# Polysketch attention and multiplicative FFN: the written order of all engines carried on to the third group's x

## The chip, the cores and the metric

One core of a Trainium2 chip runs the kernel. Its engines are TensorE (PE, matmuls and transposes), VectorE (DVE), ScalarE (ACT), GpSimd (POOL) and SyncE (SP), which here issues the DMAs. Each engine works through its own queue in order; an instruction waits in its queue until the tiles it reads are written and the buffers it writes are free. The metric is the device time of one execution in microseconds (us).

## The reference

For 4 batches, 4 heads, 1088 positions and head dimension 32, with two sketch matrices S1 and S2 of 8 x 32:

```
phi(x)[.., i*8+j] = (S1 x)[i] * (S2 x)[j]            # 64 features
kv  = sum over s of phi(k)[s] v[s];  z = sum over s of phi(k)[s]
att = (phi(q) kv) / (phi(q) z + 1e-6)
x   = att as (4*1088, 128)                            # heads side by side
out = ((x @ w1) * (x @ w2)) @ w3 @ w_out              # d_ff = 1024
```

w1, w2, w3 and w_out arrive as float64 and are read as 64-bit words; the kernel turns them into float32 itself.

## The kernel before

**Fold.** Nothing non-linear stands between w3 and w_out, so the kernel computes w3o = w3 @ w_out once and then needs only ((x @ w1) * (x @ w2)) @ w3o. w3 is 1024 x 1024 and comes in 16 chunks of 128 x 512 (two to each block of 128 rows), behind w1 and w2 (two chunks each) and w_out (two chunks). A chunk in its raw form is 512 KB; there are six buffers for raw chunks, and the step that reads chunk n issues the load of chunk n+6 on SP.

**Converting one chunk** (`convert`, L256): `words` are two ACT instructions (L269 writes cv_c, L270 writes cv_m; two buffers each), `join` two DVE instructions (L281, L282), `add` one (L285). For w3 the result is a tile w3c (three buffers). `w3_t` (L415) turns it with four PE transposes (L421) and copies them to w3T with ACT (L423). When both halves of a row block are there, `w3_mm` (L425) makes one block of w3o with eight PE matmuls (L428) and an ACT copy (L429).

**Attention side.** `k_steps(b)` makes, for batch b, the small matrices that the q side needs: a maximum and two-part split of k (`lead`: peak, first, second on DVE), two transposes and a feature product (`k_feat_by_head`: tr on DVE, ab on PE and DVE, feat on DVE), sums over positions on PE (`g_sum`, `kv_sum`, and the rest rows), then a chain of small steps in which DVE and PE alternate: fin1 (DVE), T on PE, a pair split on DVE, N on PE, a pair split on DVE, and the transposed kv block kz. `next_in` issues the loads of later batches. `q_main(b, half)` makes x for one group of 512 positions: transpose and grid on DVE, lead on ACT, rest, ay1 and ay2 on PE, then split, dens, dens2 and phi on DVE, phT (eight PE transposes L807, two ACT copies L809) and nd (PE L818, ACT copy L822 to xT).

**FFN side.** There are nine groups (eight of 512 positions, one of 256). For each of 8 chunks of 128 columns, `ffn_ab` (L858) does a = w1 x on PE (L862), its copy on ACT (L864), b = w2 x on PE (L866) and the product ab on DVE (L868). `ffn_o` (L871) adds w3o[c] ab to the group's output on PE (L875); behind the eighth, DVE transposes the result to oT (L879) and SP stores it. a, b, the w3 transposes and the w3o product share three PSUM banks (tag "h"); the output has one bank ("out"), and so have the T, N, kz, k_ab and x products ("t").

**Order.** Up to the eighth chunk of group 0 all instructions have an order written out in a list (`run_all`, L945); ordering edges on each engine make the queues follow it. Everything behind it is traced from `merge`, which mixes lists of steps by the costs written beside them, and the framework's planner then arranges each engine's instructions by its own cost estimates and by when buffers come free; all of it is behind the written part on its engine. The first such mix is group 1's FFN chunks, the K steps of batch 1 and the rest of the w3 conversion and fold; the second is the pending output products, down to four, and x of group 2 (`q_main(1, 0)`).

Of the kernel before, what the change touches and what calls it, by code (L numbers as in the profile page):

```python
# [33 lines left out]
def kernel(  # L34
# [26 lines left out]
    NC = DF // 128  # L61
# [98 lines left out]
    def load_raw(n):  # L160
        while n_raw[0] < min(n, len(chunks)):
            i = n_raw[0]
            n_raw[0] += 1
            raw[i] = io.tile([128, CW], I64, tag="raw", bufs=NRAW, name="raw")
            if i == 2:

                nc.vector.memset(raw[i].bitcast(I32)[:1, :1], 0)
            src = chunk_src(*chunks[i])
            dst = raw[i]
            if len(src.shape) == 3:  # L170
                dst = dst.rearrange("p (c d) -> p c d", d=DM)
            nc.sync.dma_start(dst, src)
# [50 lines left out]
    def halves(words, n):  # L223

        w = words.bitcast(I32)
        return bview(w, [[2, n]]), bview(w[:, 1:], [[2, n]])
# [29 lines left out]
    def convert(n, dst, signs=True):  # L256

        x = {}

        def words():
            for name in "cm":
                x[name] = work.tile([128, CW], F32, tag="cv_" + name, name="cv_" + name)
            lo, hi = halves(raw.pop(n), CW)
            nc.scalar.mul(x["c"], hi.bitcast(F32), 2.0 ** -112)  # L269
            nc.scalar.mul(x["m"].bitcast(I32), lo.bitcast(U32), 2.0 ** -29)  # L270
            load_raw(n + 1 + NRAW)
            if signs:
                x["s"] = zeros_with_signs(x["c"], 128, CW)

        def join():
            x["t"] = t = dst().bitcast(I32)
            c = x["c"].bitcast(I32)
            if signs:
                nc.vector.scalar_tensor_tensor(t, c, 3, x["s"], ALU.logical_shift_left, ALU.bitwise_or)
            else:  # L280
                nc.vector.tensor_scalar(t, c, 3, 0x7FFFFFF8, ALU.logical_shift_left, ALU.bitwise_and)  # L281
                nc.vector.scalar_tensor_tensor(t, c, -(1 << 31), t, ALU.bitwise_and, ALU.bitwise_or)  # L282

        def add():
            nc.vector.tensor_tensor(x["t"], x["t"], x["m"].bitcast(I32), ALU.add)  # L285
        return [words, join, add]

    def run_all(steps):
        for f in steps:
            f()  # L290
# [115 lines left out]
    def w_in_steps():  # L406
        return [convert(n, lambda name=name, i=i: {"w1": w1, "w2": w2}[name][:, i * CW:(i + 1) * CW])
                for n, (name, i) in enumerate(chunks) if name in ("w1", "w2")]

    def w_out_steps():  # L410

        tiles = []
        w3T, w3c = {}, {}

        def w3_t(i):  # L415
            ko, half = divmod(i, NH)
            if half == 0:
                w3T[ko] = work.tile([128, NC, 128], F32, tag="w3T", name="w3T")
            ps = psum.tile([128, CW // 128, 128], F32, tag="h", bufs=3, name="ps_wt")
            for c in range(CW // 128):  # L420
                nc.tensor.transpose(ps[:, c], w3c[i][:, c * 128:(c + 1) * 128], ident)  # L421
            c0 = half * (CW // 128)
            nc.scalar.copy(w3T[ko][:, c0:c0 + CW // 128], ps)  # L423

        def w3_mm(ko):  # L425
            ps = psum.tile([128, DM], F32, tag="h", bufs=3, name="ps_w3o")
            for c in range(NC):
                nc.tensor.matmul(ps, w3T[ko][:, c], wo[:, c], start=(c == 0), stop=(c == NC - 1))  # L428
            nc.scalar.copy(w3o[:, ko], ps)  # L429

        for n, (name, i) in enumerate(chunks):
            after = []
            if name == "wo":
                c = CW // DM
                dst = lambda i=i, c=c: wo[:, i * c:(i + 1) * c].rearrange("p c d -> p (c d)")
            elif name == "w3":
                dst = lambda i=i: w3c.setdefault(i, work.tile([128, CW], F32, tag="w3c", bufs=3, name="w3c"))
                after.append((0.5, lambda i=i: w3_t(i)))
                if i % NH == NH - 1:
                    after.append((0.9, lambda ko=i // NH: w3_mm(ko)))  # L440
            else:
                continue
            words, join, add = convert(n, dst, signs=False)
            tiles.append(([(0.6, words)], [(0.4, join), (0.3, add)], after))
        st = []
        for k in range(len(tiles) + 2):
            for part, lag in ((0, 0), (1, 1), (2, 2)):
                if 0 <= k - lag < len(tiles):
                    st += tiles[k - lag][part]
        return st  # L450

# [92 lines left out]
    def rest_steps(m):  # L546
        kf = k_rs[m]
        return k_feat(lambda: [kf.rearrange("p h d -> p (h d)")], 1, k_rest[m], "t" if m else "wb")[0]
# [277 lines left out]
    def q_main(b, half):  # L826
        def transpose(qT):
            t = by_head["q", b]
            nc.vector.transpose(qT, t[:, half * 512:(half + 1) * 512])
            if half == 1:  # L830
                nc.vector.transpose(qT_rest[:, b * SR:(b + 1) * SR], t[:, SM:])
                if b + 2 < B:
                    load_by_head("q", b + 2)
        return q_steps((b, half), transpose, lean=2 * b + half < 3)

    def q_rest():
        return q_steps("rest")
# [33 lines left out]
    def ffn_o(g, c):  # L871
        _, n, dst = groups[g]
        if c == 0:
            o_ps[g] = psum.tile([DM, 512], F32, tag="out", name="ps_o")
        nc.tensor.matmul(o_ps[g][:, :n], w3o[:, c], ab_sb.pop((g, c))[:, :n], start=c == 0, stop=c == NC - 1)  # L875
        if c == NC - 1 and g < NG - 1:

            oT = work.tile([128, 512], F32, tag="oT", name="oT")
            nc.vector.transpose(oT, o_ps[g])  # L879
            dst(oT)  # L880
# [15 lines left out]
    pend = []  # L896

    def ffn_steps(g, left):

        st = []  # L900
        if g is not None:
            for c in range(NC):
                st.append((1.7 * groups[g][1] / 512, lambda c=c: ffn_ab(g, c)))
                pend.append((g, c))
                while len(pend) > left:
                    st += o_step(*pend.pop(0))
        while len(pend) > left:
            st += o_step(*pend.pop(0))
        return st
# [6 lines left out]
    def merge(*streams):  # L916
        streams = [x for x in streams if x]
        tot = [sum(c for c, _ in x) for x in streams]
        done = [0.0] * len(streams)
        pos = [0] * len(streams)  # L920
        res = []
        while any(pos[i] < len(x) for i, x in enumerate(streams)):
            i = min((i for i, x in enumerate(streams) if pos[i] < len(x)),
                    key=lambda i: (done[i] + streams[i][pos[i]][0] / 2) / max(tot[i], 1e-9))
            res.append(streams[i][pos[i]])
            done[i] += res[-1][0]
            pos[i] += 1
        return res

    def run(steps):  # L930
        for _, f in steps:
            f()

    w_in, w_out = w_in_steps(), w_out_steps()
    fs = lambda steps: [f for _, f in steps]
    (peak, first, second, nat0, tr0, ab0, kp0, gs0, kv0, nat1, tr1, ab1, kp1, gs1, kv1, gr, kvr,
     fin1, next_in, T_mm, T_pair, N_mm, N_pair, kz) = fs(k_steps(0))
# [1 line left out]
    q_tr, q_grid, q_lead, q_rem, ay1, ay2, split, dens, dens2, phi, phT, nd = fs(q_main(0, 0))  # L939
    n_tr, n_grid, n_lead, n_rem, n_ay1, n_ay2, n_split, n_dens, n_dens2, n_phi, n_phT, n_nd = fs(q_main(0, 1))  # L940
    f = fs(ffn_steps(0, 16))
    (v0, j0, a0), (v1, j1, a1), (v2, j2, a2), (v3, j3, a3) = w_in
    pause = lambda n: lambda: idle(n)
    out_st, w_out = fs(w_out[:7]), w_out[7:]
    run_all([sk_words, sketch_pairs, nat0, nat1, peak, sketch_T, tr0, tr1, ab0, ab1, r_nat, r_tr, first, second,  # L945
             gs0, r_ab, kp0, gs1, kp1, gr, r_kp, sketch_P_mm, kv0, kv1, kvr, q_tr, pause(5),
             sketch_R, sketch_Pa, fin1, load_more, next_in, T_mm, sketch_Pb, kz, pause(13), T_pair, N_mm, q_grid, q_lead,
             pause(16), N_pair, ay1, q_rem, v0, v1, ay2, n_tr, pause(30), split, dens, dens2, phi, j0, a0, j1, a1,
             phT, nd, n_grid, n_lead, n_rem, f[0], n_ay1, n_ay2, v2, n_split, j2, a2, f[1], v3, f[2], j3, a3, n_dens, f[3],
             out_st[0], n_dens2, f[4], out_st[1], n_phi, f[5], *out_st[2:4], f[6], n_phT, n_nd, *out_st[4:7], f[7]])  # L950
    traced = nc.cur_bb.bb.instructions
    first_part = len(traced)
    run(merge(ffn_steps(1, 16), k_steps(1), w_out))
    run(merge(ffn_steps(None, 4), q_main(1, 0)))
    run(merge(ffn_steps(2, 6), q_main(1, 1), rest_steps(1) + k_steps(2)))
    run(merge(ffn_steps(3, 6), q_main(2, 0)))
    run(merge(ffn_steps(4, 6), q_main(2, 1), k_steps(3)))
    run(merge(ffn_steps(5, 6), q_main(3, 0)))
    run(merge(ffn_steps(6, 6), q_main(3, 1)))
    run(merge(ffn_steps(7, 6), q_rest()))  # L960
    run(ffn_steps(8, 2))
    run(ffn_steps(None, 0))
    last_out()
# [41 lines left out]
```

## Time and profile before

| | |
|---|---|
| three runs | 302.32, 303.18, 300.95 us; median 302.32 |
| the profiled execution | 300.8 us; span in the profile 299.0 us; mean granted clock 0.994 |
| PE | 282.7 us busy (95%), 2214 matmul instructions |
| DVE | 207.6 us (69%), 523 instructions |
| ACT | 117.1 us (39%), 226 |
| POOL | 7.5 us (3%), 12 |
| DMA | 22.37 MB |

The page's second part cuts the span into 40 slices of 7.5 us; a digit is the busy share of an engine in tenths, 9 being 90% or more. PEclk is the clock granted to PE in tenths of full speed. A line of the fifth part gives source line, engine, operation, written and read tiles with their shapes and the number of instructions, then busy time in us, mean ns of one, and the engine's idle time ahead of them with what ended most of it. A timeline line gives start and length in us, engine, source line, operation and tiles, and in brackets the idle time ahead of it and its releaser. The rows of PEld are PE's weight loads. Ends of matmuls are modelled: a pair that forms one 512-column product has 1.02 us in the timeline, while the chain of waits, which follows one start to the next, has 0.86 us for it.

### The profile page before, as it was taken

How to read it: one execution, taken by the hardware profiler on the slowest of the kernel's cores; microseconds unless marked ns; L12 is line 12 of the kernel's file. 1: busy time of each engine (PE TensorE's matmuls, PEld its weight loads, DVE VectorE, ACT ScalarE, POOL GpSimd, SP SyncE). 2: the span in 40 equal slices, each digit the busy share in tenths (PEclk: the TensorE clock that was granted, in tenths of full speed). 3: DMA queues.
4: the chain of work that ended last, by engine and by line, in shares of the span. 5: the costliest groups of instructions: out<-in, count | busy, mean ns of one | idle time of the engine just before them, and what ended most of it. 6: DMA issues, size and time to landing. Idle time of an engine off the chain costs nothing.

```text
span 299.0 us, 5582 instructions
## 1 busy us (share of the span) xinstructions
PE 282.7 (95%) x2214; PEld 159.8 (53%) x2214; DVE 207.6 (69%) x523; ACT 117.1 (39%) x226; POOL 7.5 (3%) x12
## 2 busy tenths in 40 slices
PE   7987799589999999999999999999999999999994
PEld 5876343267767774545644435464444444444572
DVE  6989779999998985699579329864862583453131
ACT  4634665667886322320242322122423323223122
POOL 0000000000000010010010001000100000000000
PEclk9999999979999999999999999999999999999999
DMA  5649996456744002200100200020002002002020
GB/s 164 211 99 311 254 309 252 134 160 201 246 123 134 0 2 35 71 2 10 30 0 0 35 2 1 2 37 0 2 0 35 2 0 35 1 2 35 0 35 18
DMA packets 28729, 22.37 MB, mean 75 GB/s; under 512 B 20000, under 2 KB 25248, under 8 KB 28704
## 3 DMA queue, kind: packets, MB, share of 16 engines
q1 hardware_dynamic: 28704, 22.03, 26.8%
q8 instruction: 17, 0.28, 0.4%
q14 instruction: 8, 0.07, 0.1%
HBM read 19.80 MB, written 2.23 MB: 74 GB/s over the span
## 4 chain that ended last, share of the span: by engine, by line
PE 80%; DVE 11%; ACT 3%; DMA 2%; issue 1%; SPq 1%; DVEq 0%
PE ps_o L875 19%; PE a_ps L862 19%; PE b_ps L866 18%; PE ps_kvz L557 5%; PE ps_w3o L428 5%; PE ps_x L818 3%; PE ps_wt L421 2%; PE ps_c L725 2%; PE ps_ph L807 2%; DMA k_sb<-in_k_dram 1%; DMA raw<-in_moe_w_dram 1%; PE ps_ab L504 1%; DVE g_k L301 1%; DVE w3c L285 1%; PE ps_c L738 1%
## 5 line engine op out<-in xcount | busy, mean ns | idle before, releaser
L868 DVE TENSOR_TENSOR ab<-ffa,b_ps 128x512 f32<-128x512 f32 (+1 forms) x72 | 47.1, 655 | 64.7 <-PE b_ps L866 62.9
L864 ACT COPY ffa<-a_ps 128x512 f32<-128x512 f32 (+1 forms) x72 | 40.4, 562 | 98.1 <-PE a_ps L862 98.0
L862 PE MATMUL a_ps<-xT,w 128*128 128x512 f32 (+1 forms) x144 | 71.9, 581 | 1.0 <-ACT xT L822 0.7
L866 PE MATMUL b_ps<-xT,w 128*128 128x512 f32 (+1 forms) x144 | 70.3, 570 | 0.0
L875 PE MATMUL ps_o<-ab,w3o 128*128 128x512 f32 (+1 forms) x144 | 70.0, 582 | 0.1
L866 PEld LDWEIGHTS b_ps<-xT,w 128*128 128x128 f32 x144 | 27.2, 190 | 30.1 <-issue 24.9
L875 PEld LDWEIGHTS ps_o<-ab,w3o 128*128 128x128 f32 x144 | 25.3, 189 | 23.9 <-issue 21.6
L862 PEld LDWEIGHTS a_ps<-xT,w 128*128 128x128 f32 x144 | 24.9, 190 | 23.5 <-issue 14.3
L809 ACT COPY pT<-ps_ph 128x512 f32<-128x512 f32 (+1 forms) x18 | 9.2, 565 | 21.0 <-PE ps_ph L807 21.0
L428 PEld LDWEIGHTS ps_w3o<-wo,w3T 128*128 128x128 f32 x128 | 16.5, 205 | 1.5 <-issue 1.2
L428 PE MATMUL ps_w3o<-wo,w3T 128*128 128x128 f32 x128 | 17.0, 289 | 0.0
L269 ACT ACTIVATE cv_c<-raw 128x512 f32<-128x512 f32 x22 | 14.9, 679 | 2.9 <-DVE w3c L282 1.5
L270 ACT ACTIVATE cv_m<-raw 128x512 int32<-128x512 uint32 x22 | 15.0, 681 | 1.8 <-DVE w3c L285 1.5
L421 PE MATMUL ps_wt<-ident,w3c 128*128 128x128 f32 x64 | 10.2, 288 | 4.7 <-DVE w3c L285 4.7
L215 PE MATMUL idle_ps<-zeros 128*128 128x256 bf16 x88 | 12.7, 309 | 1.7 <-DVE zeros L210 1.7
L822 ACT COPY xT<-ps_x 128x512 f32<-128x512 f32 (+1 forms) x9 | 5.1, 563 | 19.0 <-PE ps_x L818 19.0
L421 PEld LDWEIGHTS ps_wt<-ident,w3c 128*128 128x128 f32 x64 | 7.5, 147 | 8.7 <-ACT cv_c L269 4.2
L215 PEld LDWEIGHTS <-zeros 128*128 128x128 bf16 x88 | 9.6, 112 | 3.8 <-DVE zeros L210 1.7
L701 POOL TENSOR_TENSOR q<-qT,q 128x512 f32<-128x512 f32 x5 | 5.9, 1183 | 208.6 <-ACT q L697 208.6
L423 ACT COPY w3T<-ps_wt 128x512 f32<-128x512 f32 x16 | 9.2, 585 | 4.9 <-PE ps_wt L421 4.6
L807 PEld LDWEIGHTS ps_ph<-ident,ph 128*128 128x128 f32 x68 | 7.9, 142 | 5.8 <-issue 4.0
L285 DVE CUSTOM_DVE_ANT_0 w3c<-w3c,cv_m 128x1024 uint16<-128x1024 uint16 x16 | 10.8, 682 | 0.0
(182 smaller groups left out, 343.9 us busy)
## 6 DMA issues: line engine op xcount, KB each, us to landing
raw<-in_moe_w_dram SPq DMA_DIRECT2D x20, 512.0 KB, 5.0
qh<-in_q_dram SPq DMA_DIRECT2D x4, 544.0 KB, 5.8
k_sb<-in_k_dram SPq DMA_DIRECT2D x4, 512.0 KB, 5.2
out_dram<-oT SPq DMA_DIRECT2D x32, 64.0 KB, 1.9
kh<-in_k_dram SPq DMA_DIRECT2D x12, 128.0 KB, 6.4
v_sb<-in_v_dram SPq DMA_DIRECT2D x12, 128.0 KB, 5.1
raw<-in_moe_w_out_dram SPq DMA_DIRECT2D x2, 512.0 KB, 7.7
v_sb<-in_v_dram SPq DMA_DIRECT2D x1, 512.0 KB, 4.9
```

The source lines that it names most:

```text
L215: nc.tensor.matmul(idle_ps[:, :n], zeros[:, :128], zeros[:, :n], start=True, stop=True)
L269: nc.scalar.mul(x["c"], hi.bitcast(F32), 2.0 ** -112)
L270: nc.scalar.mul(x["m"].bitcast(I32), lo.bitcast(U32), 2.0 ** -29)
L421: nc.tensor.transpose(ps[:, c], w3c[i][:, c * 128:(c + 1) * 128], ident)
L428: nc.tensor.matmul(ps, w3T[ko][:, c], wo[:, c], start=(c == 0), stop=(c == NC - 1))
L557: nc.tensor.matmul(out[h * D:(h + 1) * D], lhs, rhs, start=start, stop=stop, skip_group_check=True)
L807: nc.tensor.transpose(ps[:, j * 128:(j + 1) * 128], s["ph"][:, j, 2 * p:2 * p + 2].rearrange("p h i j -> p (h i j)"), ident)
L862: nc.tensor.matmul(a_ps[:, :n], w1[:, cols], xT[key], start=True, stop=True)
L864: nc.scalar.copy(a_sb[:, :n], a_ps[:, :n])
L866: nc.tensor.matmul(b_ps[:, :n], w2[:, cols], xT[key], start=True, stop=True)
L868: nc.vector.tensor_mul(ab[:, :n], a_sb[:, :n], b_ps[:, :n])
L875: nc.tensor.matmul(o_ps[g][:, :n], w3o[:, c], ab_sb.pop((g, c))[:, :n], start=c == 0, stop=c == NC - 1)
```

## The change

`w_out_steps` no longer returns one flat list of steps with costs, but 21 rounds. Round k holds words of tile k (tiles 0 and 1 are w_out, 2 to 17 the chunks of w3), join and add of tile k-1, and the transposes (and, for every second chunk, the fold product) of tile k-3. The first three rounds hold the same seven steps that were in the written order before.

The written order then goes on. It runs through rounds 3 to 20 with the chunks of group 1 (g[0] to g[7]) and the output products of group 0 (o0[0] to o0[7]) between them; the K steps of batch 1 begin with k_peak behind round 12 and end with k_kz; then come the steps of `q_main(1, 0)`, with group 1's output products (o1[0] to o1[7]) between them, up to nd. Only what is behind that is left to the planner: group 2 and later ones, mixed from the same lists as before. When group 2 begins, no output product is pending, where there were four.

```diff
-            words, join, add = convert(n, dst, signs=False)
-            tiles.append(([(0.6, words)], [(0.4, join), (0.3, add)], after))
-        st = []
-        for k in range(len(tiles) + 2):
-            for part, lag in ((0, 0), (1, 1), (2, 2)):
-                if 0 <= k - lag < len(tiles):
-                    st += tiles[k - lag][part]
-        return st
+            tiles.append(convert(n, dst, signs=False) + [[f for _, f in after]])
+        rounds = []
+        for k in range(len(tiles) + 3):
+            st = [tiles[k][0]] if k < len(tiles) else []
+            if 0 < k <= len(tiles):
+                st += tiles[k - 1][1:3]
+            if k > 2:
+                st += tiles[k - 3][3]
+            rounds.append(st)
+        return rounds
...
-    out_st, w_out = fs(w_out[:7]), w_out[7:]
+    out_st = sum(rounds[:3], [])
...
+    (k_peak, k_first, k_second, k_tr0, k_tr1, k_ab, k_kp0, k_gs0, k_kv0, k_kp1, k_gs1, k_kv1, k_rg, k_rv,
+     k_fin1, k_next, k_Tm, k_Tp, k_Nm, k_Np, k_kz) = fs(k_steps(1))
+    q_tr, q_grid, q_lead, q_rem, ay1, ay2, split, dens, dens2, phi, phT, nd = fs(q_main(1, 0))
+    g = fs(ffn_steps(1, 16))
+    o0, o1 = ([lambda g=g, c=c: ffn_o(g, c) for c in range(NC)] for g in range(2))
+    pend.clear()
+    R = rounds
+    run_all([g[0], *R[3], g[1], *R[4], *R[5], g[2], *R[6], *R[7], o0[0], *R[8], g[3], *R[9], o0[1], *R[10], *R[11], o0[2],
+             g[4], *R[12], k_peak, o0[3], *R[13], k_first, *R[14], k_second, g[5], *R[15], o0[4], k_tr0, *R[16], k_tr1, k_ab,
+             *R[17], o0[5], k_kp0, *R[18], o0[6], k_gs0, k_kp1, *R[19], k_kv0, k_gs1, *R[20], k_kv1, k_rg, k_rv, o0[7],
+             k_fin1, g[6], k_next, k_Tm, o1[0], k_Tp, q_tr, q_grid, o1[1], k_Nm, q_lead, g[7], k_Np, q_rem, k_kz, o1[2], ay1, ay2,
+             split, o1[3], o1[4], dens, o1[5], dens2, o1[6], o1[7], phi, phT, nd])
     traced = nc.cur_bb.bb.instructions
     first_part = len(traced)
-    run(merge(ffn_steps(1, 16), k_steps(1), w_out))
-    run(merge(ffn_steps(None, 4), q_main(1, 0)))
-    run(merge(ffn_steps(2, 6), q_main(1, 1), rest_steps(1) + k_steps(2)))
...
+    def group(g, left, *others):
+        run(merge(ffn_steps(g, left), *others))
+
+    group(2, 6, q_main(1, 1), rest_steps(1) + k_steps(2))
```

More of the change, by code (lines that the diff above doesn't have):

```diff
@@ L932, in run @@
             f()
-    w_in, w_out = w_in_steps(), w_out_steps()
+    w_in, rounds = w_in_steps(), w_out_steps()
     fs = lambda steps: [f for _, f in steps]
@@ L950 @@
              out_st[0], n_dens2, f[4], out_st[1], n_phi, f[5], *out_st[2:4], f[6], n_phT, n_nd, *out_st[4:7], f[7]])
+    (k_peak, k_first, k_second, k_tr0, k_tr1, k_ab, k_kp0, k_gs0, k_kv0, k_kp1, k_gs1, k_kv1, k_rg, k_rv,
[10 more added lines that the diff above has]
+             split, o1[3], o1[4], dens, o1[5], dens2, o1[6], o1[7], phi, phT, nd])
     traced = nc.cur_bb.bb.instructions
     first_part = len(traced)
-    run(merge(ffn_steps(1, 16), k_steps(1), w_out))
-    run(merge(ffn_steps(None, 4), q_main(1, 0)))
-    run(merge(ffn_steps(2, 6), q_main(1, 1), rest_steps(1) + k_steps(2)))
[L956 to L960, printed above, removed]
+    def group(g, left, *others):
+        run(merge(ffn_steps(g, left), *others))
+    group(2, 6, q_main(1, 1), rest_steps(1) + k_steps(2))
+    group(3, 6, q_main(2, 0))
+    group(4, 6, q_main(2, 1), k_steps(3))
+    group(5, 6, q_main(3, 0))
+    group(6, 6, q_main(3, 1))
+    group(7, 6, q_rest())
     run(ffn_steps(8, 2))
```

## The prediction

> **What bounds the kernel now.** I read the page's slices first, then the engines in stretches of one microsecond, then the groups of instructions, then the timeline from 54 to 120 us.
>
> ```profile
> PE   7987799589999999999999999999999999999994
> DVE  6989779999998985699579329864862583453131
> ACT  4634665667886322320242322122423323223122
> PEclk9999999979999999999999999999999999999999
> ```
>
> A slice is 7.5 us. From the tenth slice on TensorE (PE) is full, so the kernel can gain only where PE still idles: up to 67 us. The stretch the change rewrites is slices 8 to 16, and there VectorE (DVE) is full too, up to slice 13. Two engines are near their limit at once.
>
> ```profile
> 56.00:57.00 1.00, 0.06 (x1) 0.00 (x0) 1.00 (x4) 0.94 (x2) 0.00 (x0) 1.00 0.82 307
> 57.00:58.00 1.00, 0.00 (x0) 0.00 (x0) 1.00 (x4) 0.07 (x1) 0.00 (x0) 1.00 0.13 45
> 58.00:59.00 1.00, 0.00 (x0) 0.00 (x0) 1.00 (x2) 0.60 (x1) 0.00 (x0) 1.00 0.78 221
> 59.00:60.00 1.00, 0.63 (x4) 0.42 (x4) 1.00 (x3) 0.79 (x2) 0.00 (x0) 1.00 0.72 291
> 60.00:61.00 1.00, 0.00 (x0) 0.00 (x0) 1.00 (x3) 0.93 (x2) 0.00 (x0) 0.98 0.14 29
> 61.00:62.00 1.00, 0.91 (x5) 0.91 (x5) 1.00 (x2) 0.69 (x1) 0.00 (x0) 0.50 0.77 217
> ```
>
> Columns: stretch, length, busy PE, weight loads, DVE, ACT, POOL, granted clock, DMA share, GB/s. Right behind the hand-ordered part PE has a hole from 56.05 to 61.09 us with 0.63 us of work in it, and the clock is then 0.50 to 64 us: the first fold product took 2.88 us in the chain of waits, a later one 1.78. This 4.4 + 1.1 = 5.5 us is what a better order could win here.
>
> Prices come from the groups:
>
> ```profile
> L428 PE MATMUL ps_w3o<-wo,w3T 128*128 128x128 f32 x128 | 17.0, 289 | 0.0
> L269 ACT ACTIVATE cv_c<-raw 128x512 f32<-128x512 f32 x22 | 14.9, 679 | 2.9 <-DVE w3c L282 1.5
> L423 ACT COPY w3T<-ps_wt 128x512 f32<-128x512 f32 x16 | 9.2, 585 | 4.9 <-PE ps_wt L421 4.6
> L285 DVE CUSTOM_DVE_ANT_0 w3c<-w3c,cv_m 128x1024 uint16<-128x1024 uint16 x16 | 10.8, 682 | 0.0
> ```
>
> and the end of the stretch from the timeline:
>
> ```profile
> 115.78 1.04 PE L807 MATMUL ps_ph<-ident,ph 128*128 128x128 f32 x8
> 116.42 1.07 ACT L809 COPY pT<-ps_ph 128x512 f32<-128x512 f32 x2 [6.32 <-PE ps_ph L807]
> 116.55 0.30 PEld L875 LDWEIGHTS ps_o<-ab,w3o 128*128 128x128 f32 x2
> 116.66 1.02 PE L875 MATMUL ps_o<-ab,w3o 128*128 128x512 f32 x2
> 117.61 1.08 PE L818 MATMUL ps_x<-pT,kz 128*64 128x512 f32 x4
> 118.62 1.12 PE L875 MATMUL ps_o<-ab,w3o 128*128 128x512 f32 x2
> 118.76 0.59 ACT L822 COPY xT<-ps_x 128x512 f32<-128x512 f32 x1 [1.27 <-PE ps_x L818]
> 119.58 0.30 PEld L862 LDWEIGHTS a_ps<-xT,w 128*128 128x128 f32 x2
> ```
>
> Around each copy of the x chain (L809, L822) the planner has put an output product (L875), so PE does not wait.
>
> **What the Trainium skill says.** "TensorE: Matmul & The Clock Gate", Part 1, says the PE clock drops to half after about 3.4 us of idleness and recovers after about 3.4 us of work; the hole above and the 0.50 behind it agree. The same page (engine queue depths) says ACT and DVE are strict FIFO: an instruction that waits holds all behind it. "VectorE: DVE Perf Modes", The DRAIN you can't avoid, has a next op wait until the pipe is empty, earlier if it is not held. Here L282 behind the L281 it reads starts 0.45 us later (50.17 to 50.62), L281 with foreign work behind it is followed after 0.33 (56.44 to 56.77). "Perfetto Trace Analysis", Identifying the Most-Contended Engine, warns that matmul busy share misleads; so I count PE by chain durations below.
>
> **The change, part by part.** Units. PE: an a or b product 0.86, four transposes of a w3 tile (T) 0.44, fold product (mm) 1.78, output product (o) 0.86. ACT, start to start: two conversion steps (words) 1.14, w3T copy 0.50, ffa copy 0.49, w3o copy 0.17. DVE: join and add 0.45 + 0.72 + 0.61 = 1.78, ab product 0.61. PE's end to ACT's start 0.2, other hand-overs 0.1, b product start to DVE 1.13 (65.78 to 66.91).
>
> *PE content.* From 56.05 to the third group's first a product the new order issues 16 T (7.0), 8 mm (14.2), g1 to g7 (7 x 1.72 = 12.0; g0 ran at 54.2), 16 o (13.8), and K sums, their rest rows, T, N, kz, ay, phT and nd (about 11.8, read as gaps in the chain): 58.9 us. Without idling it ends at 114.9. The kernel before reaches that product at 119.6, but with 4 output products (3.4) still pending and 1.05 us of group 3's K sums done. Parity is 119.6 + 3.4 - 1.05 = 122.0. **So 7.1 us of PE idling is break-even.**
>
> *Removed*: the hole and its cold clock, 5.5 us, replaced by g1 and g2, which need only xT and three PSUM banks.
>
> *Added: strict order between the engines.* Each round has words k on ACT, join and add k-1 on DVE, T k-3 on PE and its copy on ACT behind words k. cv_c and cv_m have two buffers, so words k waits for join and add k-2; behind it stand the w3T copy, the w3o copy and the ffa copy. PE waits for those: the second half of mm needs the copy, g needs mm, DVE's ab needs g, the next join stands behind ab. I walked this by hand. Rounds 9 to 12: ab of g3 on DVE at 72.1; join 8 done 73.9, so words 10 at 74.0 to 75.3; T5's copy to 75.9 though T5 ended at 73.6; mm2 stops half way from 74.5 to 75.95, ends 76.8; T6, o, then g4 76.8 to 80.0 with 0.1 us for w3o; ab of g4 at 80.25. That is 8.1 us with 3 T, mm, 2 o and g = 6.5 us of PE and three joins and ab = 6.0 us of DVE. 1.6 us of PE and 2.1 us of DVE idle. At 78.3 us the walk has done 16.2 us of PE work since 56.05, 6.0 us idle.
>
> Milestones on: mm3 ends 82.5, mm4 87.9, mm5 94.6 (k_ab then waits for two DVE transposes, 0.8), mm6 100.0, mm7 106.7, o0[7] 109.5. At that point 42.2 of 53.4 us are work: **11 us idle**. Low bound: DVE alone, never waiting, is done with the last join at 95 and o0[7] ends near 102; with joins at 0.33 + 0.61 + 0.61 = 1.55, as if nothing in them depended, at 92 and near 99, which is PE's own pace. No gain beyond that: PE's 42.2 us are all needed. High bound: the walk and some cold clock, rival 3.
>
> *Moved: the K chain from under the conversion to behind it.* Before, fin1 began at 91.8 under FFN and fold work. Now DVE does peak, first and second (1.2 + 1.2 + 1.2), two transposes, k_ab and two kp (1.4 + 0.7 + 2.4) between late joins, and fin1 behind o0[7] and its oT: 0.2 + 0.65 + fin1 2.0 (112.3); T_mm and pair to 114.65; N_mm to 115.5; g7's ab at 117.5 stands ahead of N's pair on DVE, done 119.4; kz, one o, ay1 to 120.95 (kz shares ps_N's bank, so PE stands from 117.2 to 119.4); ay2 1.8 to 122.75; o1[3] to o1[7] until 127.05 while split, dens and dens2 (5.1) end at 126.0. phi stands behind oT of the second group: 127.25 + 0.65 + 1.25 = 129.15. phT 0.87, pT's copy, nd to 131.6, xT's copy, first a product **132.5**. All 16 output products are spent by then, so nothing covers these copies, and on every engine all later work stands behind. About 6 us of the tail are PE idle.
>
> *SyncE and POOL.* raw loads stay with words, six ahead, 5.0 us to landing: no wait. K and V loads of the fourth batch and kh of the third leave 69 to 90 us for about 113, behind four out stores that wait for oT; kh is first read in the third group (after 132; 6.4 us to land), the others later: nothing, and raw loads get DMA to themselves. q(1,0) is lean, so POOL gets nothing from it.
>
> *Third group*: it starts with no pending products, and DVE has all of q(1,1) and K 2 left (about 28 us against 25.5 of PE). The group after it leaves DVE room (busy 9.25 of 20 us from 160 to 180) and can take the K part, so 0; up to 3 us if PE waits.
>
> *Sum*: 132.5 - 122.0 = +10.5 on the profiled 299.0 span, 309.5; with the 1.8 us around it 311.3 against 300.8. That run lies 1.5 us under the median 302.3, so **312.8**.
>
> **Rivals.**
> 1. *PE sets the pace* (ends faster). If the joins take 1.55 and words find their buffers free, PE runs mm after mm, as from 65 us before, 5.8 us a pair of tiles (64.9, 70.7, 76.4). Place: the wait of words on join k-2. Price: the 11 us shrink to 1; with 3 of the tail's 6 left, 302.3 - 7.1 + 4 = 299.2. It decides at 7.1 us of idling in all. For: hole gone, 3.4 us of FFN done early. Against: the tail's idling alone is about 6.
> 2. *DVE alone sets the pace*: o0[7] at 102, tail as walked: 125.0, +3, 305.3. For: DVE's full slices. Against: ACT's copies stand behind words.
> 3. *The clock gate trips again*: PE pauses of 2 us side by side leave windows too empty; four times 1.1 us: 317.
> 4. *The change does nothing*: order edges do not bind. Then 302.3. Against: the first part runs in the written order already.
>
> **How the numbers follow.** Forecast 0.62 (307 to 316), rival 1 0.09, rival 2 0.20 (303 to 307, half of it over 1%), rival 3 0.07, rival 4 0.02. Slower by over 1% (305.3, about what a measurement tells from no change): 0.62 + 0.07 + 0.10 = 0.79. Within 1%: 0.10 + 0.02 + 0.01 of rival 1 = 0.13. Faster 0.08. The range leaves out rivals 1 and 4 and the far end of 3: 303 to 318.
>
> **What the profile after would show.** Right: no hole of 3 us behind 56 and clock 1.00 at 61; fold products whose second half waits for w3T (L423), ACT's L423 behind L269 and L270; DVE idle before L868 in 60 to 80; last L285 near 102; fin1 near 110; PE holes of about 2 us ahead of kz and of phT; first a product of the third group near 132. Wrong: last L285 before 96 (rival 2), PE slices full from 56 to 130 (rival 1), clock 0.5 in them (rival 3). The forecast fails most easily in the walk, if PSUM banks or copies come free in another order than I assumed.

## The result, and the profile after

The changed kernel takes 313.35 us (median of four executions, 313.06 to 315.36), the kernel before 302.19 beside it: a ratio of 1.0386, 95% interval 1.0327 to 1.0444. The profiled execution took 313.15 us with a span of 311.4; the span before was 299.0.

Line numbers behind L409 are one to three higher than before: the transposes of w3 (T) are L422, their copy L424, the fold product (mm) L429, its copy L430, a and b L865 and L869, the ffa copy L867, the ab product L871, the output product (o) L878, the output transpose L882. Experiments that move the copy ahead of words add two more (o is L880 there).

The page's slices, 7.8 us each:

```profile
PE   7987899788988995799999999999999999999994
DVE  6989789886798276889986944966592393363131
PEclk9999999999999999999999999999999999999999
```

The dip of the clock in the ninth slice is gone. In its place PE is short of full in most slices from 8 to 17, where before it was full from the tenth on, and DVE has lost its run of nines. Stretches of one microsecond behind the old end of the written order (length, busy PE, weight loads, DVE, ACT, POOL, clock, DMA share, GB/s):

```profile
56.00:57.00 1.00, 1.00 (x4) 0.52 (x4) 0.78 (x2) 1.00 (x2) 0.00 (x0) 1.00 0.87 344
57.00:58.00 1.00, 0.91 (x3) 0.08 (x1) 0.93 (x2) 0.59 (x2) 0.00 (x0) 1.00 0.15 53
58.00:59.00 1.00, 0.25 (x2) 0.25 (x3) 1.00 (x2) 0.94 (x2) 0.00 (x0) 1.00 0.86 217
...
61.00:62.00 1.00, 0.12 (x1) 0.00 (x0) 0.97 (x3) 0.96 (x3) 0.00 (x0) 1.00 0.98 340
```

Here the hole of 5 us has become two of about 1 us, and the clock stays at 1.00. More waits follow; those of rounds 10 to 12 in the timeline:

```profile
73.67 1.06 PE L429 MATMUL ps_w3o<-wo,w3T 128*128 128x128 f32 x8
74.04 0.69 ACT L269 ACTIVATE cv_c<-raw 128x512 f32<-128x512 f32 x1 [0.53 <-ACT w3T L424]
74.77 0.67 ACT L270 ACTIVATE cv_m<-raw 128x512 int32<-128x512 uint32 x1
75.35 0.57 ACT L424 COPY w3T<-ps_wt 128x512 f32<-128x512 f32 x1
75.97 1.16 PE L429 MATMUL ps_w3o<-wo,w3T 128*128 128x128 f32 x8 [1.25 <-ACT w3T L424]
80.43 0.69 DVE L871 TENSOR_TENSOR ab<-ffa,b_ps 128x512 f32<-128x512 f32 x1 [1.97 <-PE b_ps L869]
```

Words (L269, L270) keep the w3T copy waiting, that copy stops the fold product half way, the FFN chunk behind it comes late, and DVE waits 1.97 us for b. The words of the next join are done at 78.56, but that join stands behind ab in DVE's queue. At the end of the written part:

```profile
109.20 1.12 PE L878 MATMUL ps_o<-ab,w3o 128*128 128x512 f32 x2
116.78 0.72 ACT L699 ACTIVATE q<-qT,g_q 128x512 f32<-128x512 f32 x1 [4.97 <-DVE g_q L297]
118.16 0.57 ACT L867 COPY ffa<-a_ps 128x512 f32<-128x512 f32 x1
118.76 0.69 DVE L871 TENSOR_TENSOR ab<-ffa,b_ps 128x512 f32<-128x512 f32 x1 [2.02 <-ACT ffa L867]
120.67 0.33 PE L660 MATMUL ps_kz<-ident,kvm 128*128 128x128 f32 x1 [3.14 <-DVE Nb L323]
128.18 0.72 DVE L882 STREAM_TRANSPOSE oT<-ps_o 128x512 f32<-128x512 f32 x1 [0.80 <-PE ps_o L878]
128.82 1.25 DVE L801 TENSOR_TENSOR ph<-ay,bs 128x512 f32<-128x512 f32 x2
129.61 1.39 PE L810 MATMUL ps_ph<-ident,ph 128*128 128x128 f32 x8 [1.47 <-DVE ph L801]
131.24 1.56 PE L821 MATMUL ps_x<-pT,kz 128*64 128x512 f32 x4 [0.24 <-ACT pT L812]
133.64 1.02 PE L865 MATMUL a_ps<-xT,w 128*128 128x512 f32 x2
```

The first line is o0[7]. PE stands 3.14 us ahead of kz and 1.47 ahead of phT. The third group begins at 133.64 us; before, at 119.58, with four output products still to come.

### The profile page after: what moved, and what is told of

The parts are those of the page before. It is cut to its first block, busy times and chain, and to the rows that moved or that the text cites. A ratio compares the mean times of both kernels' runs of the same rounds, so it can differ in the third digit from the quotient of the medians.

```text
span 311.4 us, 5588 instructions
## 1 busy us (share of the span) xinstructions
PE 286.1 (92%) x2214; PEld 157.8 (51%) x2214; DVE 212.4 (68%) x523; ACT 115.7 (37%) x226; POOL 7.9 (3%) x12
## 4 chain that ended last, share of the span: by engine, by line
PE 67%; DVE 20%; ACT 6%; issue 3%; DMA 1%; SPq 1%; DVEq 0%; ACTq 0%
PE ps_o L878 17%; PE a_ps L865 16%; PE b_ps L869 16%; PE ps_kvz L560 4%; PE ps_x L821 3%; DVE ab L871 3%; PE ps_w3o L429 2%; PE ps_c L728 2%; DVE w3c L282 2%; PE ps_ph L810 2%; DMA k_sb<-in_k_dram 1%; PE ps_ab L507 1%; DVE w3c L281 1%; DVE ph L801 1%; ACT cv_c L269 1%
## 5 line engine op out<-in xcount | busy, mean ns | idle before, releaser
L871 DVE TENSOR_TENSOR ab<-ffa,b_ps 128x512 f32<-128x512 f32 (+1 forms) x72 | 47.2, 655 | 63.0 <-PE b_ps L869 59.3
L867 ACT COPY ffa<-a_ps 128x512 f32<-128x512 f32 (+1 forms) x72 | 40.4, 562 | 97.7 <-PE a_ps L865 95.6
L865 PE MATMUL a_ps<-xT,w 128*128 128x512 f32 (+1 forms) x144 | 72.0, 582 | 1.0 <-ACT xT L825 0.7
L878 PE MATMUL ps_o<-ab,w3o 128*128 128x512 f32 (+1 forms) x144 | 70.2, 585 | 0.7 <-ACT w3o L430 0.7
L869 PE MATMUL b_ps<-xT,w 128*128 128x512 f32 (+1 forms) x144 | 70.2, 569 | 0.0
L869 PEld LDWEIGHTS b_ps<-xT,w 128*128 128x128 f32 x144 | 27.3, 190 | 31.0 <-issue 25.8
L865 PEld LDWEIGHTS a_ps<-xT,w 128*128 128x128 f32 x144 | 25.1, 191 | 25.2 <-issue 15.1
L878 PEld LDWEIGHTS ps_o<-ab,w3o 128*128 128x128 f32 x144 | 24.9, 190 | 21.9 <-issue 18.6
L429 PE MATMUL ps_w3o<-wo,w3T 128*128 128x128 f32 x128 | 17.8, 283 | 4.5 <-ACT w3T L424 4.1
L429 PEld LDWEIGHTS ps_w3o<-wo,w3T 128*128 128x128 f32 x128 | 15.5, 191 | 6.4 <-ACT w3T L424 5.9
L269 ACT ACTIVATE cv_c<-raw 128x512 f32<-128x512 f32 x22 | 14.9, 678 | 2.4 <-DVE w3c L282 1.3
L270 ACT ACTIVATE cv_m<-raw 128x512 int32<-128x512 uint32 x22 | 14.8, 671 | 0.2
L810 PE MATMUL ps_ph<-ident,ph 128*128 128x128 f32 x68 | 9.4, 276 | 3.2 <-DVE ph L801 3.0
L422 PEld LDWEIGHTS ps_wt<-ident,w3c 128*128 128x128 f32 x64 | 7.5, 141 | 8.4 <-issue 4.4
L422 PE MATMUL ps_wt<-ident,w3c 128*128 128x128 f32 x64 | 9.7, 277 | 2.1 <-ACT w3T L424 1.2
L424 ACT COPY w3T<-ps_wt 128x512 f32<-128x512 f32 x16 | 9.3, 580 | 6.3 <-PE ps_wt L422 6.3
```

What stands on the lines that cost most here:

```text
L810: nc.tensor.transpose(ps[:, j * 128:(j + 1) * 128], s["ph"][:, j, 2 * p:2 * p + 2].rearrange("p h i j -> p (h i j)"), ident)
L865: nc.tensor.matmul(a_ps[:, :n], w1[:, cols], xT[key], start=True, stop=True)
L867: nc.scalar.copy(a_sb[:, :n], a_ps[:, :n])
L869: nc.tensor.matmul(b_ps[:, :n], w2[:, cols], xT[key], start=True, stop=True)
L871: nc.vector.tensor_mul(ab[:, :n], a_sb[:, :n], b_ps[:, :n])
```

## The experiments

A ratio is that to the kernel before, run on the same chip; "changed" is the changed kernel.

**e1: leave the tail to the planner.** The written order ends behind o0[7].

```diff
-             k_fin1, g[6], k_next, k_Tm, o1[0], k_Tp, q_tr, q_grid, o1[1], k_Nm, q_lead, g[7], k_Np, q_rem, k_kz, o1[2], ay1, ay2,
-             split, o1[3], o1[4], dens, o1[5], dens2, o1[6], o1[7], phi, phT, nd])
+             ])
     traced = nc.cur_bb.bb.instructions
     first_part = len(traced)
+    pend.extend((1, c) for c in range(4, NC))
+    chain = k_main[14:] + q_main(1, 0)
+    run(merge([(1.7, g[6]), (0.85, o1[0]), (0.85, o1[1]), (1.7, g[7]), (0.85, o1[2]), (0.85, o1[3])], chain))
```

> The written order ends behind o0[7]; fin1 to x of the third group, the last two chunks of group 1 and its output products go to the planner, four products left pending as in the kernel before. Theory A (order couples the engines, and the uncovered tail costs about 6 us beside the conversion): the kernel before changed by the conversion stretch alone, 6 to 8 us less than the changed kernel, 305.5 to 307.5. Rival B (the conversion at VectorE's pace makes the whole loss, the tail is a dependent chain that any order pays): within 2 us of 313.4. The stretch up to o0[7] must look the same in both, o0[7] near 109.

Measured 316.65 us (315.61 to 317.96), 1.0486 [1.0436, 1.0535]: slower than with the tail written by hand, and neither expectation. o0[7] starts at 109.80 against 109.20, so the conversion is the same. DVE's timeline shows what the planner did with the chain, and PE's what came of it:

```profile
117.48 1.34 DVE L301 TENSOR_REDUCE g_k<-k_sb 128x1 f32<-128x1152 f32 x1
...
123.51 1.21 DVE L301 TENSOR_REDUCE g_k<-k_sb 128x1 f32<-128x1024 f32 x1
...
125.26 0.28 PE L716 MATMUL ps_a<-Rh,q 128*128 128x64 bf16 x4 [1.76 <-DVE Rh L655]
133.74 2.06 PE L810 MATMUL ps_ph<-ident,ph 128*128 128x128 f32 x8 [5.90 <-DVE ph L801]
```

It put maxima and splits of later batches between the short steps of the chain, phi came 4 us later, and PE stood 5.9 us. The clock had dropped to half before that, at about 126.9 us, and was 0.64 in the mean from 130 to 140 us. So the planner did not cover this late K chain either; as its time also holds a cold stretch of some 10 us, the run does not price its order alone.

**e2: the copy ahead of words.** In each round T and its copy first, the fold product last.

```diff
-            st = [tiles[k][0]] if k < len(tiles) else []
+            st = tiles[k - 3][3][:1] if k > 2 else []
+            if k < len(tiles):
+                st.append(tiles[k][0])
             if 0 < k <= len(tiles):
                 st += tiles[k - 1][1:3]
             if k > 2:
-                st += tiles[k - 3][3]
+                st += tiles[k - 3][3][1:]
```

> In each round the transposes of tile k-3 and their ScalarE copy stand ahead of words k, the fold product stays behind add. Theory A: the second halves of the fold products no longer wait for a copy behind words (5 to 6 us of such waits in the changed kernel); some comes back as VectorE waiting for words: 3 to 6 us less, 307.5 to 310.5. Rival B (VectorE's joins set the pace): within 1 us of 313.4.

Measured 313.89 us (310.64 to 315.12), 1.0372 [1.028, 1.0463]: no change in the median, as rival B has it. But o0[7] starts at 106.40, 2.8 us earlier. The stretches of the profiled execution (columns as above) show where that went:

```profile
116.00:118.00 2.00, 0.12 (x1) 0.13 (x2) 1.82 (x10) 0.00 (x0) 0.00 (x0) 1.00 0.94 231
118.00:120.00 2.00, 2.00 (x13) 1.43 (x14) 1.44 (x6) 0.27 (x1) 0.00 (x0) 0.85 0.09 21
120.00:122.00 2.00, 2.00 (x12) 2.00 (x11) 1.35 (x4) 0.00 (x0) 0.00 (x0) 0.50 0.00 0
122.00:124.00 2.00, 2.00 (x5) 0.97 (x5) 1.49 (x5) 0.00 (x0) 0.00 (x0) 0.50 0.00 0
124.00:126.00 2.00, 2.00 (x4) 0.97 (x3) 1.32 (x5) 0.00 (x0) 0.00 (x0) 0.50 0.00 0
```

Behind the wait for kz the clock was at half for some 7 us. The four executions line up by mean clock: 310.64 us at 0.999, 313.70 at 0.987, 314.08 at 0.986, 315.12 at 0.975. The one at full clock is 2.4 to 2.9 us under the changed kernel's three at 0.998 and 0.999, so the order itself gains, if less than theory A's 3 to 6 us.

**e3: four conversion buffers.** To make room, the buffers of ab go from 18 to 14.

```diff
-                x[name] = work.tile([128, CW], F32, tag="cv_" + name, name="cv_" + name)
+                x[name] = work.tile([128, CW], F32, tag="cv_" + name, bufs=4, name="cv_" + name)
-        ab = work.tile([128, 512], F32, tag="ab", bufs=LAG + 2, name="ab")
+        ab = work.tile([128, 512], F32, tag="ab", bufs=LAG - 2, name="ab")
```

> The changed kernel with four buffers for cv_c and cv_m in place of two (ab's from 18 to 14 to make room). Words k no longer wait for join and add k-2. Theory A, its term as the prediction put it (words held by the buffers, the copies behind them): the waits of words for a join that stand in the changed kernel's trace, 0.3 + 1.0 + 0.5 + 0.6 us, and the fold products behind them shrink: 1 to 3 us less, 310.5 to 312.5. Rival (the copies stand behind words whatever these wait for; strict order alone, not the buffers): within 1 us of 313.4.

Measured 311.96 us (310.37 to 315.01), 1.0362 [1.0293, 1.0431]. The interval does not settle it. At a clock of 0.998 it took 310.37 and 310.75, where the changed kernel took 313.15 and 313.55, and o0[7] starts at 106.80, 2.4 us earlier: the buffers held words, as theory A has it, for about that much.

**e4: another hand order of the tail.**

```diff
-             *R[17], o0[5], k_kp0, *R[18], o0[6], k_gs0, k_kp1, *R[19], k_kv0, k_gs1, *R[20], k_kv1, k_rg, k_rv, o0[7],
-             k_fin1, g[6], k_next, k_Tm, o1[0], k_Tp, q_tr, q_grid, o1[1], k_Nm, q_lead, g[7], k_Np, q_rem, k_kz, o1[2], ay1, ay2,
-             split, o1[3], o1[4], dens, o1[5], dens2, o1[6], o1[7], phi, phT, nd])
+             *R[17], o0[5], k_kp0, *R[18], o0[6], k_gs0, k_kp1, *R[19], k_kv0, k_gs1, *R[20], k_kv1, k_rg, k_rv, k_fin1, o0[7],
+             g[6], k_next, k_Tm, o1[0], k_Tp, q_tr, q_grid, o1[1], k_Nm, g[7], q_lead, k_Np, q_rem, o1[2], o1[3], ay1, ay2, k_kz,
+             split, o1[4], dens, o1[5], dens2, phi, o1[6], phT, o1[7], nd])
```

> The tail stays written by hand but in another order: fin1 ahead of o0[7], q_lead behind g[7], kz behind ay2, phi ahead of the last output products, one product each between phi, phT and nd. The conversion is untouched. Theory A: the wait of kz (3.1 us), of g[7]'s product behind q_lead (1.2) and the holes around phi and phT (2 to 3) shrink: 4.5 to 6.5 us less, 307 to 309. Rival B (dependent chain): within 1.5 us of 313.4.

Measured 310.88 us (310.19 to 312.57), 1.0301 [1.025, 1.0351]: 2.5 us less, below the expected gain. The third group starts at 130.08 against 133.64; the wait of kz is gone, but PE still stands 1.38 us for phi, as the products that should cover it were spent ahead:

```profile
125.95 1.39 PE L810 MATMUL ps_ph<-ident,ph 128*128 128x128 f32 x8 [1.38 <-DVE ph L801]
130.08 1.02 PE L865 MATMUL a_ps<-xT,w 128*128 128x512 f32 x2
```

**e5: the kernel before, with three more steps written.**

```diff
-             out_st[0], n_dens2, f[4], out_st[1], n_phi, f[5], *out_st[2:4], f[6], n_phT, n_nd, *out_st[4:7], f[7]])
+             out_st[0], n_dens2, f[4], out_st[1], n_phi, f[5], *out_st[2:4], f[6], n_phT, n_nd, *out_st[4:7], f[7],
+             g[0], *fs(w_out[:3]), g[1]])
...
-    run(merge(ffn_steps(1, 16), k_steps(1), w_out))
+    run(merge(g_all[2:], k_steps(1), w_out[3:]))
```

> The kernel before, its written order carried on by three things only: g[0], round 3 and g[1]; everything else planned as before. Theory A (what an order could win is the hole from 56 to 61 us and the cold clock behind it): the hole shrinks by g[1]'s 1.7 us and the clock stays full, 2 to 4 us faster than before, 298 to 300. Rival B (VectorE's pace holds the fold, PE's hole costs nothing): 302, no change.

Measured 300.65 us over 20 executions (298.58 to 302.56), 0.9967 [0.9944, 0.999]. Smaller than expected: the hole moved. PE waited 2.04 us for the next T at 64.78, and the clock fell behind it (a line of the timeline, then stretches):

```profile
64.78 0.63 PE L421 MATMUL ps_wt<-ident,w3c 128*128 128x128 f32 x4 [2.04 <-ACT cv_c L269]
65.00:66.00 1.00, 1.00 (x11) 1.00 (x10) 1.00 (x3) 0.93 (x2) 0.00 (x0) 0.93 0.06 16
66.00:67.00 1.00, 1.00 (x6) 1.00 (x6) 1.00 (x1) 0.03 (x1) 0.00 (x0) 0.50 0.34 45
67.00:68.00 1.00, 1.00 (x7) 1.00 (x5) 1.00 (x3) 0.00 (x0) 0.00 (x0) 0.50 0.93 340
```

At a mean clock of 1.000 it took 298.58 to 298.92 us, at 0.980 301.98 to 302.56. Not all of this difference belongs to the moved hole. The same trace has a second cold stretch from about 11.3 to 14.7 us, ahead of everything that e5 changes; the trace of the kernel before does not have it:

```profile
12.00:13.00 1.00, 1.00 (x32) 0.93 (x22) 1.00 (x2) 0.00 (x0) 0.00 (x0) 0.50 0.33 115
```

**e6: e2 and e4 together.** Against e2:

```diff
-             *R[17], o0[5], k_kp0, *R[18], o0[6], k_gs0, k_kp1, *R[19], k_kv0, k_gs1, *R[20], k_kv1, k_rg, k_rv, o0[7],
+             *R[17], o0[5], k_kp0, *R[18], o0[6], k_gs0, k_kp1, *R[19], k_kv0, k_gs1, *R[20], k_kv1, k_rg, k_rv, k_fin1, o0[7],
...
```

with the tail's lines as in e4.

> Both edits at once: transposes and copy ahead of words, and the tail in the other written order (e2 and e4). In e2 the conversion ended 2.8 us earlier, but TensorE then paused 3.1 us for kz and ran at half clock from about 117 to 125 us, which took it back. Theory: without that pause the clock stays full and the two gains add: 313.4 - 2.8 - 2.5 to 3.5 = 307 to 308.5. Rival (e2's order gains nothing in itself, the later chain takes it): 310 to 311.5, as e4.

Measured 308.42 us (307.52 to 309.73), 1.0236 [1.0198, 1.0273]. The two gains add once the wait of 3 us for kz, and the cold stretch behind it, are gone.

**e7: the K chain into the conversion.** The rounds of e2; fin1 now behind round 16, nine output products kept back.

```diff
+    run_all([g[0], *R[3], g[1], *R[4], *R[5], g[2], *R[6], *R[7], o0[0], *R[8], k_peak, k_first, g[3], *R[9], o0[1],
+             *R[10], *R[11], o0[2], k_second, k_tr0, g[4], *R[12], k_tr1, k_ab, o0[3], *R[13], k_kp0, k_gs0, *R[14],
+             k_kp1, k_kv0, g[5], *R[15], k_gs1, o0[4], *R[16], k_kv1, k_rg, k_rv, k_fin1, *R[17], o0[5], k_Tm, *R[18],
+             o0[6], k_Tp, q_tr, q_grid, k_next, g[6], k_Nm, *R[19], q_lead, k_Np, q_rem, g[7], *R[20], k_kz, ay1, ay2,
+             o0[7], split, o1[0], o1[1], dens, o1[2], dens2, o1[3], phi, o1[4], o1[5], phT, o1[6], nd, o1[7]])
```

> Order still written by hand to the same point, copy ahead of words, but the K chain of batch 1 begins behind round 8, in VectorE's waits, fin1 stands behind round 16, and nine output products are kept for the chain of x. Theory C (the loss is the K chain's place behind the conversion and the fold work used up by then, not hand order as such): 300 to 306, the third group's first product near 120 to 126 us. Rival D (any strict order over three engines loses as much; the planner's mixing is what counts): 309 or more.

Measured 305.62 us (304.65 to 306.92), 1.0154 [1.0114, 1.0194]: as theory C, against rival D. Its trace still has three plain waits:

```profile
82.57 1.06 PE L509 MATMUL ps_ab<-kT,S12blk 128*32 128x256 f32 x12 [1.92 <-DVE kT L503]
97.28 0.19 DVE L301 TENSOR_REDUCE g_pair<-ps_kvz 128x1 f32<-128x32 f32 x1 [1.72 <-PE ps_kvz L562]
113.81 0.72 DVE L884 STREAM_TRANSPOSE oT<-ps_o 128x512 f32<-128x512 f32 x1 [4.25 <-PE ps_o L880]
124.83 1.02 PE L867 MATMUL a_ps<-xT,w 128*128 128x512 f32 x2
```

**e8: those waits moved.**

```diff
-             *R[10], *R[11], o0[2], k_second, k_tr0, g[4], *R[12], k_tr1, k_ab, o0[3], *R[13], k_kp0, k_gs0, *R[14],
-             k_kp1, k_kv0, g[5], *R[15], k_gs1, o0[4], *R[16], k_kv1, k_rg, k_rv, k_fin1, *R[17], o0[5], k_Tm, *R[18],
-             o0[6], k_Tp, q_tr, q_grid, k_next, g[6], k_Nm, *R[19], q_lead, k_Np, q_rem, g[7], *R[20], k_kz, ay1, ay2,
-             o0[7], split, o1[0], o1[1], dens, o1[2], dens2, o1[3], phi, o1[4], o1[5], phT, o1[6], nd, o1[7]])
+             *R[10], *R[11], o0[2], k_second, k_tr0, k_tr1, g[4], *R[12], k_ab, o0[3], *R[13], k_kp0, k_gs0, *R[14],
+             k_kp1, k_kv0, g[5], *R[15], k_gs1, o0[4], *R[16], q_tr, q_grid, k_kv1, k_rg, k_rv, k_fin1, *R[17], o0[5],
+             k_Tm, q_lead, *R[18], o0[6], k_Tp, q_rem, k_next, g[6], k_Nm, *R[19], k_Np, *R[20], k_kz, ay1, ay2,
+             split, o0[7], g[7], dens, o1[0], o1[1], dens2, o1[2], phi, o1[3], phT, o1[4], nd, o1[5]])
+    pend.extend((1, c) for c in (6, 7))
```

> The order of e7 with the holes that its trace shows moved: both transposes of k ahead of round 12 (TensorE stood 1.9 us for the second), q_tr and q_grid in VectorE's 1.7 us wait before fin1, split ahead of the output transpose it stood behind (VectorE idle 4.3 us), g[7] behind ay2; two output products left pending. Theory C: the third group's first product comes 2 to 4 us earlier than in e7 (124.8) at the same content: 301 to 303.5, level with the kernel before. Rival D (strict order itself costs about 4 us, as e7 is over the kernel before): 305 to 307.

Measured 301.55 us over 20 executions, 1.0003 [0.9981, 1.0025]: level with the kernel before, in strict order over all engines up to nd. An output product stands in each gap of the x chain again:

```profile
116.35 1.38 PE L812 MATMUL ps_ph<-ident,ph 128*128 128x128 f32 x8 [1.16 <-DVE ph L803]
117.57 1.02 PE L880 MATMUL ps_o<-ab,w3o 128*128 128x512 f32 x2
118.53 1.08 PE L823 MATMUL ps_x<-pT,kz 128*64 128x512 f32 x4
119.53 1.12 PE L880 MATMUL ps_o<-ab,w3o 128*128 128x512 f32 x2
```

Level is not free. The hole of 5 us is down to a pause of 0.84 us in e8 and the clock is 1.00 behind it. The prediction prices the hole and its cold clock at 5.5 us, so strict order still costs about that much elsewhere, an estimate from these two figures; no run takes it away.

**e10: e8 with the changed kernel's rounds** (words first again).

```diff
-            st = tiles[k - 3][3][:1] if k > 2 else []
-            if k < len(tiles):
-                st.append(tiles[k][0])
+            st = [tiles[k][0]] if k < len(tiles) else []
             if 0 < k <= len(tiles):
                 st += tiles[k - 1][1:3]
             if k > 2:
-                st += tiles[k - 3][3][1:]
+                st += tiles[k - 3][3]
```

> e8 with the rounds of the changed kernel: words ahead of the transposes and their copy again. If the copies' place behind words costs by itself, as e2's conversion (o0[7] 2.8 us earlier) says: 1.5 to 4 us above e8, 303 to 305.5. If it cost only because VectorE had nothing but joins to do there, which e8's order has mended: within 1 us of 301.6.

Measured 304.91 us (303.68 to 306.07), 1.0102 [1.0048, 1.0156], 3.4 us over e8: the copy's place behind words costs by itself. Two of the four executions had a lower clock; the two at 0.998 and 1.000 took 303.68 and 304.02, some 2.5 us over e8's at 1.000 (301.07 to 301.58). That is what e2's order gained at full clock too.

**e11: e8 with e3's buffers.**

```diff
-                x[name] = work.tile([128, CW], F32, tag="cv_" + name, name="cv_" + name)
+                x[name] = work.tile([128, CW], F32, tag="cv_" + name, bufs=4, name="cv_" + name)
-        ab = work.tile([128, 512], F32, tag="ab", bufs=LAG + 2, name="ab")
+        ab = work.tile([128, 512], F32, tag="ab", bufs=LAG - 2, name="ab")
```

> e8 with four buffers of cv_c and cv_m (ab's 14). If words' wait for join k-2 is still a limit: 299 to 301. If VectorE, over 0.94 busy from 70 to 100 us in e8, is the limit by now: within 1 us of 301.6.

Measured 301.49 us, 0.9992 [0.9967, 1.0017]: nothing. In this order the words' buffers no longer set the end.

**e9: e5 with PE kept busy.** The 16 matmuls multiply zeros into a bank that nothing reads.

```diff
-             g[0], *fs(w_out[:3]), g[1]])
+             g[0], *fs(w_out[:3]), g[1], fill])
+    def fill():
+        ps = psum.tile([128, 256], F32, tag="wb", name="fill_ps")
+        for _ in range(16):
+            nc.tensor.matmul(ps, zeros[:, :128], zeros, start=True, stop=True)
```

> e5 (the kernel before with g[0], round 3 and g[1] in the written order) with 16 matmuls on zeros behind g[1], in which nothing is computed: TensorE is busy 1.7 us longer there. In e5 the time follows the granted clock, 298.6 at 1.000 and 302.2 at 0.980. If that is the clock gate behind the hole of 2.0 us at 62.7, the fill keeps the clock at 1.0 in most executions: 298.5 to 300. If the fill only delays the fold: 301 to 302.5.

Measured 299.23 us (298.74 to 300.53), 0.9914 [0.9879, 0.995]: 0.9% under the kernel before. The clock stays full in the stretches where e5's was at half (again behind a line of the timeline):

```profile
63.92 0.63 PE L421 MATMUL ps_wt<-ident,w3c 128*128 128x128 f32 x4 [1.35 <-ACT cv_c L269]
65.00:66.00 1.00, 1.00 (x11) 1.00 (x10) 1.00 (x2) 0.17 (x1) 0.00 (x0) 1.00 0.53 49
66.00:67.00 1.00, 0.93 (x37) 0.72 (x35) 1.00 (x3) 0.34 (x2) 0.00 (x0) 1.00 0.82 299
67.00:68.00 1.00, 1.00 (x10) 0.82 (x12) 1.00 (x3) 0.97 (x2) 0.00 (x0) 1.00 0.44 176
```

The fill closes the first pause, and as PE's work behind it comes later, the second one shrinks from 2.04 to 1.35 us. At a clock of 0.999 and 1.000 it takes 298.74 to 299.23 us, as e5 at 1.000: what it gains is clock.

## Why the prediction was right

The forecast was 312.8 us, the measurement 313.35. That the two lie this close is in part luck. Against the profiled execution the forecast was 311.3, and that execution took 313.15. Of the 1.9 us between them, 1.1 had come by the start of the third group, the rest behind it. The 1.5 us that were added on top, because the profiled execution of the kernel before lay that far under its median, made up for most of this; in the changed kernel the two are 0.2 us apart. Its steps:

*The hole and its cold clock go.* Right: T0 starts at 58.75, the first fold product at 62.86, the clock is 1.00.

*Strict order couples the engines.* Right in place, and in size by the forecast's own count. The ab of g3 starts at 72.20 (walk: 72.1), words 10 at 74.04 (74.0), mm2 stops until 75.97 (75.95), ab of g4 at 80.43 (80.25). o0[7] ends at 109.20 + 0.86 = 110.06 (109.5), which leaves 54.0 - 42.2 = 11.8 us of idling (11). This is the measured end less the forecast's price of the work. The trace itself has PE busy for 46.5 of the 54.0 us, so idle for 7.5; whether the rest is work priced too low or the modelled ends of matmuls at each stop is not shown. e2, e3 and e10 show the two causes that the step named: 2.8 us of that stretch for the copy behind words, 2.4 for the two buffers; e10 puts the copy's place at 3.4 in another order, 2.5 at full clock. They don't add up to 11.8.

*What the step left out* is what DVE could do there: its queue held only ab products and joins. e7 and e8 put the K steps into those waits and come out at 1.0154 and level; what strict order still costs is then about the 5.5 us that the hole had cost. The larger part of the loss against the kernel before is thus the place of the K chain, of the steps of x and of the output products, which e7, e8 and e10 move together and no run separates: e10, with words first, is 8.4 us under the changed kernel; putting the copy first gives the other 3.4. The sum is not in doubt, but its split into "11 of coupling and 6 of tail" described where PE stood, not what could be mended.

*K chain behind the conversion.* Right: fin1 starts at 111.01, the third group at 133.64 (132.5). The idling of the tail is 133.64 - 110.06 - (58.9 - 42.2) = 6.9 us (6); by PE's busy time in the trace it is 5.9. Its one mis-sized term is g7: the walk had ab at 117.5, it came at 118.76, because q_lead stood ahead of the ffa copy on ACT and waited for DVE's grid until 116.78. The sentence that "nothing covers these copies" as all products are spent held too. Theory A of e1, that the planner would cover them, did not hold: the chain takes 23 us and only 16.7 us of PE work are left beside it. Another hand order, e4, brings the third group 3.6 us earlier.

*SP and POOL.* The loads of later batches moved to about 115 us (DMA share 1.05 from 115 to 120) and no wait for one of them stands in the timeline. Right.

*Third group at nothing.* The span grew by 12.4 us. The start of the third group accounts for 133.64 - 122.0 = 11.6; 0.8 came later, inside the stated 0 to 3.

*Rivals.* PE's pace (1) and DVE's alone (2) did not come; the last join ended at 102.5, not 96. The cold clock (3) was not in the profiled execution, but one of four had a mean clock of 0.987 and took 315.36, and it weighs in e1 and e2.

## What to carry to other kernels

Before writing an order by hand, list for each engine what it can do in the other engines' waits: a long chain of small alternating steps belongs under the bulk work, started early, with some independent matmuls held back for its last copies. In a strict queue, put the copy that the busiest engine waits for ahead of work that only fills buffers. A fix of one stall is worth what the next wait leaves of it, so read the granted clock along with the time.

## What was not expected of the hardware

A pause of the same length gave two clocks. The changed kernel's 3.14 us ahead of kz left the clock at 1.00 in the profiled execution; e2's 3.14 us at the same step left it at 0.50 for some 7 us. The Trainium skill, "TensorE: Matmul & The Clock Gate", Part 1, says that the activity window of about 3.4 us runs freely; this fits, as does e5, where one program took 298.6 to 302.6 us with mean clocks from 1.000 to 0.980. The lengths of the cold stretches fit too. Worked out from the granted clock of the stretches around them, they are 3.4 us in the kernel before and twice in e5, 6.8 in e2 and 10.2 in e1: whole windows.

A pause need not reach 3.4 us to cost, so the 3.4 us of idleness that the prediction took from that page are no safe limit here. In e1 the clock fell behind a wait of 1.76 us. In e5 it fell behind pauses of 0.84 and 2.04 us with 2.4 us of work between them; which of the two was needed is not shown. Sixteen idle matmuls, on PE from 58.51 to 60.25 us in e9, left one pause of 1.35 us. The median was 1.4 us under e5's; the two were measured on different chips, and the intervals of their ratios, [0.9944, 0.999] and [0.9879, 0.995], overlap a little.
